# Single-pass warm-up products and a new hand-written order for the first phase of an mLSTM and mixture-of-experts kernel

## The chip, the core and the metric

The kernel runs on one core of a Trainium2 chip. The metric is device time in microseconds (us) of one execution; lower is better. One execution was taken apart by the hardware profiler, and all rows below come from it. The engines are named as the profile names them: PE (TensorE matmul), PEld (its weight loads, which overlap PE), DVE (VectorE), ACT (ScalarE), POOL (GpSimd) and SP (SyncE, which here only starts DMA transfers). SPq and POOLq are the queues on which these two start transfers.

## The reference

Three layers follow each other. The first is a gated recurrent attention (mLSTM) over 4 batches, 8 heads, 768 positions and head size 40; the second is a plain feed-forward layer over the 3072 tokens; the third sends each token to one of 8 experts.

```python
def _attn_ref(q, k, v, i_gate, f_gate, o_gate):      # B, H, S, D = 4, 8, 768, 40
    for t in range(S):
        m_new = np.maximum(f_gate[:, :, t] + m, i_gate[:, :, t])
        f_stab = np.exp(f_gate[:, :, t] + m - m_new)
        i_stab = np.exp(i_gate[:, :, t] - m_new)
        C = f_stab * C + i_stab * np.einsum('bhd,bhe->bhde', vt, kt)
        n = f_stab * n + i_stab * kt
        h_tilde = np.einsum('bhde,bhe->bhd', C, qt)
        denom = np.maximum(np.abs(nq), 1.0)          # nq = n . qt
        y[:, :, t] = o * h_tilde / denom             # o = sigmoid(o_gate)

def _moe_ref(x, w_in, w_out, alpha):                 # 3072 x 320 -> 2048 -> 320
    h = x @ w_in
    g = np.maximum(h, 0.0) + alpha * np.minimum(h, 0.0)
    return g @ w_out

def _moe2_ref(x, w_gate, w_output_gate, w1, w2):     # 8 experts, 320 -> 1024 -> 320
    e_idx = np.argmax(x @ w_gate, axis=1)            # one expert for each token
    for e in range(E):
        h = np.maximum(x[mask] @ w1[e], 0.0)
        out[mask] = gate_w[mask, None] * eom[mask, e, None] * (h @ w2[e])
```

## The kernel before

**First phase.** The attention is worked in 24 units: 4 batches times 6 chunks of 128 positions. A unit has about a dozen steps: loads of q, k, v and gates, the scores (`att_s`, on PE from `q` and `k`), their masking by `D` (`att_e` on ACT and POOL), the product with the values (`att_b`), the reading and the update of the running state (`att_h`, `att_d`), the division (`att_y`) and the transposition into `xTs` (`att_c`). Every three units fill a block of 384 tokens. A block then runs through the feed-forward layer in 16 slices of 128 hidden columns: `ffn1` (code F, eight products of 384 columns), the two-sided activation on ACT and DVE, `ffn_split` (code g, a copy on ACT and a subtraction on DVE), and `ffn2` (code S, nine products of 336 columns into three accumulators). There are 8 blocks, so 128 of each of F, g and S. Full precision comes from splitting a number into a high and a low half and multiplying them one by one.

Beside this the first phase decodes and splits the feed-forward weights (`dec_*`, `split_*`, `gate_w`), and reads the 64 pieces of the expert weights, splits them and stores both halves in the DRAM tensor `scr` (`expert_load`, `expert_split`, `expert_store`). Near its end it picks the expert of each token (`block_out`, `block_out2`), stores the rows in the DRAM tensor `x1d`, and sorts the tokens by expert (`route_*`), which gives `tok`, the list of rows for each slot of 128 tokens, and `roff`, the place of each slot's weights.

**Second phase.** Some 28 slots of 128 tokens follow (`slot_x`, `slot_1`, `slot_t`, `slot_2`, `slot_out`). Each gathers its rows from `x1d` by an indirect DMA on POOL and multiplies them by one expert's weights, which lie in the large buffer `ring`. The same buffer holds the feed-forward weights in the first phase, so the 33 `early_load` steps (code ld) bring the first three experts into parts of it as these come free. Slot 0 is worked inside the first phase (`first_rows`, `first_x`, `first_1`, `first_t`, `first_2`), since its rows are known from the first seven blocks; `first_set` clears its row buffer, which is one of the five buffers of the tag `D`. The slots from 1 on need the rows of all blocks in `x1d`, the whole of `tok`, and `roff`.

**What sets the order.** Nothing is scheduled by the compiler there. `ORDER` (lines 85 to 124) is a string of 1399 codes; each code calls the next step of its kind, and its instructions are put at the end of the queues of the engines it uses. Every engine, and SP for the transfers, works strictly in that order, so a step that waits holds up all that stands behind it on the same engine. The tables in `OTHER` say for which numbers of a step a subtraction or multiplication goes to the other of DVE and POOL.

**Warm-up products.** `warm` (line 1138) is a PE product whose result nobody reads. It multiplies `ident` by 512 columns of the constants `cst` in float32, which PE works in four passes. There are 14: three near the start, six a little later, and five single or paired ones before the first F.

Of the kernel before, what the change touches and what calls it, by code (L numbers as in the profile page):

```python
# [11 lines left out]
I32 = mybir.dt.int32  # L12
# [36 lines left out]
        0, 1, 2, 4, 5, 6, 7, 8, 11, 12, 15, 16, 17, 18, 19, 21, 23,  # L49
    ),  # L50
    "prep_kt": (
        0, 1, 2, 3, 9, 10, 12, 13, 15, 16, 21, 22,
    ),
    "att_y": (
        5, 6, 8, 9, 11, 12, 14, 16, 17, 20, 21,
    ),
# [6 lines left out]
    "split_wi": (  # L63
        0, 1, 2, 7, 9, 10, 15,
    ),
    "split_wo": (
        3, 4, 11, 13, 15,
# [18 lines left out]
lo gates_d load_gates do load_cst do load_gates lo load_wg gates pq do lo do do gw lv log do so so lg pq pq pq  # L86
pq warm warm warm gates_e do li li load_g load_g gates lk do gw di do gv pq di ae so warm warm warm warm warm
warm gates_e gw di load_sel di di lq si li di di load_g ae lg pt lo gv as as ab si load_g di do di lv sg do ay
do si gv lq lo el do li ae ad pt gw do ay do lk warm gates_d ah ay so so es gw lo di gv load_g ae do di ay ae lv
load_g ae as as do di do lq lq ah ad pt ab lk ac so ay ay ay si et ay lo as as do ah do lo gv do load_gates  # L90
gates gw warm gw ab do gv ay li lk do ay ac so lg ay gv ay lg do so di warm gw warm warm gates_e di lo ac do do
load_g load_g ae ae di si set_al1 el pq es load_g do ae lv ad lk pt as as F F load_g g ah ab gv so gw lo gates_d
li di di gv lq et g do do lv do so di si ad F log F lo do gw li di S do do g lv S so ah g lq gw di di si ay li
di di F F lg lg di S g g S ay load_g load_g pk pk lo do do as do sg si so li di F lo pt gw pk pk di di ae pt do
do pk gv ay ay si F ad ad g S g do li li di di gv S di S ah si gv di di di gw F so g pq load_g li di di gv si as
di li di S di ah li ae di lq lk F F si ab as lo do S si el g g do di do di ae as load_g ae ae di li ac es F ay
ay ay ay so F g S gw g ab ay ay ay log si di di gv li pq di ac di di S S di ay lv pt sg si lk lg si as as F ad
et load_g load_g load_g g S lk lk lo do do do ac lo lq do log do el el ae so lg do ab ay F so F gw pk as ae as
lv lv g S ay el g es pt gv load_g ae gw et el es es ay ay F F ah ad ae gv pk S pk g lq ac load_g et et S g bo F
F g es lq pq ab S g el el load_g load_g ae ae as lk ay as ay S bp F g F pk pk ah lg ab es et et S S g es F F g  # L100
as ay load_g pt S lv S lg ay ay g ad pt lk F el as pk es lq lq ac g S ae ae load_g F g lq S S F pq et el es et
ay ah ad F lv pt ab el as g g S sg load_g load_g es ay ay ah F g et F S g lk pt el as pq el pk ad ay et F S g el
ay S ac F g es et ab ay ay ay ae ae ay F F es es S S lg g lv load_g ah ah el as et g lk lv el S bo F as g ay et
es ac pq pk S lk F g load_g F ab ay ay et S g lq es et log ae F F load_g S S g el bp S ae g el el as F lv lg g
ac S lk lg lg F g F as S ae g pq pt es et S ay ay ay es F g F S S ad ad log g pt F ah pk sg es ad ab load_g F et
g ah ae S g as S lq lg lg as pq et F g lv el ac F ay es S S g el es pk ae load_g ay ay load_g F ay et et g S S
bo el el F lk ac es es ae el ab S pt et g as as pk es lq et F S F lv g g ad lq el ab pq F F S el et g g es S es
ah S ae load_g load_g lv et el ae ae F g F g ay ay ay el S pt ad pt load_g F F g S et lk ay es load_g g as F as
pk sg S g es ac pq pt S lk el ab F g et et load_g ay ay es F ay S lk g F lq ay S ay el el ae es ae ah as g et et
el F es et S g S ac lg el bp F F es as ad g pk es S g ae S S bo el ab ah lv load_g load_g et et lk lg el el F g  # L110
load_g F S g es F log pq F et g S g S bp lq F g es es ay el ah as ay et et ae ay S S F as pk F g g ay ay ae ab
pq F F lq S S S g g el F ac g F el es lv lv sg ay S ay lg es g F pt lg S g ay ac ay ay S et es F et et ay as ae
log g F as pq pk el lk el el S S S ac g F g ad ad pt es et es ab F F S g g ay et as ah es ay load_g ay S bo ay
ae F F S S g g ac el es et load_g lg el es S load_g et F ae as el g lq S F g F ad g es ab ay ay pq lk pk el sg S
S F F S g ay as et g el es load_g load_g S lv lv ae as ay et lk pt ah et es F pk S F load_g g g ae ad ab el es F
g ay S lq pq ay ay F el S et el es lq g pt load_g load_g ac F et ay F et ah ae as as pk S pq g g ab el el ac lv
bp ay F lq S g es ad F S et es F S g g S load_g es et et el bo F g F ae S S S g ae S ay lk ay ay lg lg el es pt
# [1167 lines left out]
```

## Time and profile before

| what | value |
| --- | --- |
| median of 3 runs | 833.61 us (832.91 to 836.97) |
| the profiled execution | 830.8 us, of which 829.0 us are its span |
| PE busy | 782.5 us, 94% of the span |
| PEld busy | 734.1 us, 89% |
| DVE busy | 466.8 us, 56% |
| ACT busy | 399.0 us, 48% |
| POOL busy | 265.0 us, 32% |
| mean granted clock of PE | 0.953 of full speed |

Busy time is a mean over a start-up of some 90 us, a long middle, the change between the phases at about 558 to 600 us, and the second phase. A busy PE is not PE at full speed: the granted clock has two levels, 2.4 GHz (1.00 in the rows) and 1.2 GHz (0.50), and a row between them is a stretch with both. The profile's chain of work that ended last is only two short pieces on POOL here, so the order of events is read from the timeline and the waits.

### The profile page before, as it was taken

Reading aid. Unit: us, or ns where it says so; the run is one execution under the profiler, and the core shown is the slowest. Engines: PE = TensorE matmul, PEld = TensorE weight load, DVE = VectorE, ACT = ScalarE, POOL = GpSimd, SP = SyncE. Lnnn points to the kernel's source line nnn. Section 1 sums busy time; section 2 is a strip of 40 time slices with the busy share of each in tenths; the row PEclk is TensorE's granted clock in tenths of the full one; section 3 lists DMA queues with packets and bytes.
Section 4 is the critical chain, followed back from the end, with each engine's and each line's share of the span. In section 5 each row is a group of like instructions: output and inputs, shape, how many; then the busy total and the mean of one; then the engine's idle time right before and its main releaser. Section 6 shows DMA issues by size and latency. Waiting matters only on the chain. (4 is left out here: it accounts for less than half of the span.)

```text
span 829.0 us, 15173 instructions
## 1 busy us (share of the span) xinstructions
PE 782.5 (94%) x4819; PEld 734.1 (89%) x4819; DVE 466.8 (56%) x1137; ACT 399.0 (48%) x859; POOL 265.0 (32%) x274
## 2 busy tenths in 40 slices
PE   5999999998999999999999999997699999999995
PEld 2897999998999998999998899996599999989994
DVE  5767889775767765757777576854223232323231
ACT  2624665746666757557666564331233232323331
POOL 1224233334444444354236342100222121212221
PEclk9657999999999999999999999997799999999998
DMA  7747658879799998996987976986554662771100
GB/s 221 238 145 222 190 152 283 284 229 303 238 317 287 287 292 265 308 307 235 292 264 250 304 274 240 317 319 235 183 204 183 231 266 88 293 291 30 41 13 19
DMA packets 84272, 189.45 MB, mean 229 GB/s; under 512 B 8786, under 2 KB 39567, under 8 KB 82914
## 3 DMA queue, kind: packets, MB, share of 16 engines
q1 hardware_dynamic: 80802, 179.74, 65.9%
q0 software_dynamic: 3392, 8.71, 3.3%
q8 instruction: 44, 0.72, 0.4%
q14 instruction: 34, 0.28, 0.1%
HBM read 267.71 MB, written 55.59 MB: 390 GB/s over the span
## 5 line engine op out<-in xcount | busy, mean ns | idle before, releaser
L830 PE MATMUL ph<-ring 128*128 128x384 f32 x1024 | 202.7, 345 | 7.6 <-DVE ring L846 7.2
L830 PEld LDWEIGHTS ph<-ring 128*128 128x128 f32 x1024 | 179.3, 191 | 11.8 <-DVE ring L846 11.1
L858 PE MATMUL acc<-ring 128*128 128x336 f32 x384 | 122.9, 325 | 2.2 <-ACT ring L845 1.5
L859 PE MATMUL acc<-ring 128*128 128x336 f32 x384 | 119.6, 317 | 0.0
L839 DVE SCALAR_TENSOR_TENSOR ph<-v,al,ph 128x384 f32<-128x384 f32 x128 | 78.2, 617 | 61.5 <-ACT v L838 60.7
L290 PE MATMUL po<-ring,hh 128*128 (+1 forms) x448 | 99.2, 308 | 1.2 <-DMA ring<-scr 1.0
L290 PE MATMUL p<-ring,xh 128*128 (+1 forms) x336 | 97.0, 412 | 0.6 <-issue 0.6
L1087 POOL TENSOR_TENSOR er<-er,ring 128x768 fp32r<-128x768 f32 (+1 forms) x39 | 67.7, 1742 | 92.2 <-ACT ring L1086 82.8
L390 DVE TENSOR_SCALAR yo<-po,xg 128x320 f32<-128x320 f32 x27 | 14.9, 551 | 143.6 <-PE po L290 143.6
L846 DVE TENSOR_TENSOR ring<-ph,ring 128x384 fp32r<-128x384 f32 x128 | 70.6, 555 | 40.9 <-ACT ring L845 39.0
L838 ACT ACTIVATE v<-ph 128x384 f32<-128x384 f32 x128 | 61.7, 486 | 60.0 <-PE ph L830 59.5
L845 ACT ACTIVATE ring<-ph 128x384 fp32r<-128x384 f32 x128 | 62.0, 488 | 55.7 <-DVE ph L839 52.4
L391 POOL DMA_INDIRECT out_dram<-yo,tok x28 | 28.5, 1019 | 168.9 <-DVE yo L390 161.7
L861 PE MATMUL acc<-ring 128*128 128x336 f32 x384 | 80.3, 317 | 0.0
L290 PEld LDWEIGHTS po<-ring,hh 128*128 128x128 f32 x448 | 75.8, 187 | 4.1 <-ACT hr L358 1.4
L290 PEld LDWEIGHTS p<-ring,xh 128*128 128x128 f32 x336 | 63.7, 197 | 13.9 <-issue 1.0
L858 PEld LDWEIGHTS acc<-ring 128*128 128x128 f32 x384 | 72.3, 188 | 4.0 <-ACT ring L845 2.1
L372 ACT ACTIVATE hh<-p 128x512 fp32r<-128x512 f32 x56 | 30.5, 597 | 89.0 <-PE p L369 89.0
L859 PEld LDWEIGHTS acc<-ring 128*128 128x128 f32 x384 | 72.2, 188 | 0.0
L358 ACT ACTIVATE hr<-p 128x512 f32<-128x512 f32 x56 | 33.6, 600 | 74.9 <-PE p L290 70.1
L290 PE MATMUL po<-ring,hl 128*128 (+1 forms) x224 | 69.1, 309 | 0.3 <-DVE hl L373 0.3
L1086 ACT ACTIVATE ring<-er 128x768 fp32r<-128x768 f32 (+1 forms) x64 | 50.0, 788 | 29.5 <-DMA er<-in_ew_dram 11.8
(193 smaller groups left out, 1307.9 us busy)
## 6 DMA issues: line engine op xcount, KB each, us to landing
ring<-scr SPq DMA_DIRECT2D x28, 3072.0 KB
ring<-scr SPq DMA_DIRECT2D x28, 2560.0 KB
ring<-scr SPq DMA_DIRECT2D x33, 512.0 KB
D<-gd SPq DMA_DIRECT2D x48, 256.0 KB
er<-in_ew_dram SPq DMA_DIRECT2D x32, 384.0 KB
scr<-ring SPq DMA_DIRECT2D x32, 384.0 KB
scr<-er SPq DMA_DIRECT2D x32, 384.0 KB
er<-in_ew_dram SPq DMA_DIRECT2D x32, 320.0 KB
```

Of the source, the lines that this page charges most:

```text
L290: mm = T.matmul(o_, lhsT, r, start=start, stop=stop)
L358: A.activation(hr[:, hf * 512 : (hf + 1) * 512], ph, AF.Relu)
L830: T.matmul(ph[:, :384], wi_[i][lo][:, wc], xTs[n % 2][:, xc], start=(a == 0), stop=(a == len(PASSES) - 1),)
L838: A.activation(v, ph[:, :384], AF.Relu, scale=-1.0)
L839: V.scalar_tensor_tensor(ph[:, :384], v, al1[:, i : i + 1], ph[:, :384], ALU.mult, ALU.add)
L845: A.activation(gh, v, AF.Copy)
L846: V.tensor_tensor(gl, v, gh.bitcast(F32), ALU.subtract)
L858: T.matmul(ac, gh[:, sl], hi, start=(i == 0), stop=False)
L859: T.matmul(ac, gh[:, sl], lo, start=False, stop=False)
L861: T.matmul(accs[n][t][:, :NO], gl[:, t * P : (t + 1) * P], hi, start=False, stop=(i == NFC - 1))
L1086: A.activation(eh[:, :n], st[:, :n], AF.Copy)
L1087: engine(G, V, "expert_split", x).tensor_tensor(st[:, :n].bitcast(F32R), st[:, :n], eh[:, :n].bitcast(F32), ALU.subtract)
```

## The change

Two things are changed. `warm` multiplies two parts of a region of `ring` that is cleared once by POOL at the start. The region is the first 640 columns of `xt_odd`, which the first phase writes only with its fourth unit; the type is float32r, which PE works in one pass. There are 23 such products in place of 14. And `ORDER` and `OTHER` are written anew: all 1399 steps and nine more `warm`, in another order.

```diff
 OTHER = {
     "expert_split": (
-        0, 3, 8, 12, 15, 20, 23, 28, 29, 32, 34, 37, 38, 41, 43, 44, 45, 46, 47, 53, 56, 58, 59, 60, 62,
+        0, 6, 7, 8, 11, 12, 14, 15, 16, 19, 21, 23, 25, 27, 30, 33, 34, 35, 36, 37, 39, 41, 43, 48, 49,
+        50, 52, 54, 55, 57, 58, 59, 61, 62, 63,
     ),
     "prep_q": (
-        3, 4, 5, 6, 7, 9, 10, 11, 12, 16, 17, 18, 19, 20, 21, 22, 23,
+        3, 4, 5, 6, 7, 11, 12, 15, 16, 22, 23,
     ),
...
 ORDER = """
-lo gates_d load_gates do load_cst do load_gates lo load_wg gates pq do lo do do gw lv log do so so lg pq pq pq
...
-ld ld ld ld ld route_c ld ld first_t ld first_2 ld ld ld bp route_d
+pq lo do do do pq lk lo gates_d ah load_gates load_cst do do do lv gw warm load_gates load_wg gates warm warm lo
...
+first_x ld ld S S ld ld bo ld ld ld bp first_1 first_t route_b route_c ld first_2 ld es es route_d et et ld ld
...
-    "warm": ("warm", zip(range(14))),
+    "warm": ("warm", zip(range(23))),
...
+        odd0 = carved[0]
         xt_odd = carve(5, 384)
...
+        idle = ring[:, odd0 : odd0 + 5 * P]
+        G.memset(idle.bitcast(I32), 0)
+
         def warm(i):
 
-            T.matmul(ps_h(f"warm_{i}"), ident, cst[:, :512], start=True, stop=True)
+            T.matmul(ps_h(f"warm_{i}"), idle[:, :P], idle[:, P:], start=True, stop=True)
```

The other tables of `OTHER` change in the same way. Counted over the whole program, DVE takes over from POOL 10 of the subtractions of `expert_split`, 6 of `prep_q`, 3 of `prep_k`, 4 of `split_wi` and 2 of `split_wo`, and gives it 2 of `prep_kt` and 2 of `att_y`. Lines behind 428 move down by three, and behind 1138 by six.

At the start, on SP's queue, in the kernel before (`D` is the decay matrix loaded from `gd`, `gd<-G` stores its source once DVE has made `G` for the second part of the gates, `k_0` and `q_0` are the first unit's operands):

```order
L687 DMA D_0_172<-gd 128x4x128
L687 DMA D_1_174<-gd 128x4x128
L516 DMA gd<-G_177 32x256
L456 DMA k_0_190<-in_ks_dram 40x1024
L1132 DMA sel<-in_selc_dram 32x360
L449 DMA q_0_248<-in_qs_dram 40x1024
```

The same place now:

```order
L519 DMA gd<-G_137 32x128
L578 DMA r_wo_153<-in_wo_dram 128x640
L452 DMA q_0_155<-in_qs_dram 40x1024
L690 DMA D_0_157<-gd 128x4x128
L578 DMA r_wi_159<-in_wi_dram 128x768
L690 DMA D_1_161<-gd 128x4x128
L578 DMA r_wi_169<-in_wi_dram 128x768
L452 DMA q_1_171<-in_qs_dram 40x1024
L519 DMA gd<-G_174 32x256
```

The loads of `q_0` and (further up) `k_0` stood behind the second store to `gd`; now they stand ahead of it.

At the end of the first phase, on PE, before (`acc` are the accumulators of `ffn2`, so the first two rows end the last S; `xt` is the transposition of slot 0's gathered rows `x`, `ranks` is `route_b`, `p_0_0` is `first_1`):

```order
L861 MATMUL acc_1_5739<-ring 128x336
L861 MATMUL acc_2_5740<-ring 128x336
L338 MATMUL xt_6206<-cst,x_5796 128x128 x3
L994 MATMUL ranks<-rb,cst 128x32
L999 MATMUL ranks<-oh_all,cst 128x24
L999 MATMUL ranks<-oh_all,cst 128x16
L999 MATMUL ranks<-oh_all,cst 128x8
L1004 MATMUL ranks<-oh_all,cst 128x24
L290 MATMUL p_0_0_6223<-ring,xh_6210 128x512 x3
```

The same place now, where `ph` is the last F:

```order
L833 MATMUL ph_6160<-ring 128x384 x8
L340 MATMUL xt_6180<-cst,x_3580 128x128 x3
L861 MATMUL acc_0_5775<-ring 128x336
L862 MATMUL acc_0_5775<-ring 128x336
L861 MATMUL acc_1_5776<-ring 128x336
```

The transposition of slot 0's rows stood behind the last S; now the last two S stand behind it. The `ranks` products stand behind `first_1` and `first_t` now.

On DVE, in the same stretch, before (`tok` is written by `route_c`, `hl` belongs to `first_t`, `ex`, `sm`, `z`, `zs` and `xr` to the last `block_out2`, whose rows then go to `x1d`):

```order
L988 TENSOR_TENSOR tok<-rb 128x31
L373 TENSOR_TENSOR hl_6302<-p_0_0_6303,hh_6301 128x512
L373 TENSOR_TENSOR hl_6302<-p_0_1_6310,hh_6301 128x512
L894 TENSOR_TENSOR ex_6346<-lg_6185,mx_6198 128x24
L897 TENSOR_REDUCE sm_6349<-ex_6346 128x3
L899 TENSOR_TENSOR z_6351<-lg_6185,oh_all 128x24
```

And now, where `oh_all` is the last result of `block_out`:

```order
L889 TENSOR_TENSOR oh_all<-q_7_6227,m_7_6230 128x24
L897 TENSOR_TENSOR ex_6236<-lg_6212,mx_6225 128x24
L900 TENSOR_REDUCE sm_6239<-ex_6236 128x3
L902 TENSOR_TENSOR z_6241<-lg_6212,oh_all 128x24
L904 TENSOR_REDUCE zs_6243<-z_6241 128x3
```

`block_out2` stood behind the whole of `route_c` and `first_t`; now it follows `block_out` at once, and `first_t` and `route_c` come after it.

## Rows read from the trace of the kernel before

**Rows 1.** Windows: length, busy by engine (instructions), PE clock, DMA share, GB/s.

```profile
40.00:60.00 20.00, 20.00 (x87) 18.10 (x86) 13.30 (x34) 3.80 (x12) 4.34 (x7) 0.50 0.43 137
...
100.00:540.00 440.00, 426.98 (x2795) 417.62 (x2795) 309.64 (x737) 270.91 (x582) 174.03 (x168) 1.00 0.85 272
...
560.00:580.00 20.00, 14.39 (x84) 12.40 (x85) 8.09 (x39) 3.20 (x7) 1.37 (x6) 0.74 0.62 232
...
600.00:829.00 229.00, 218.73 (x1334) 200.86 (x1333) 64.63 (x131) 68.81 (x129) 54.27 (x53) 0.99 0.41 152
```

**Rows 2.** Waits of PE over the span: in total us, times, longest us.

```profile
PE ph L830 <- DVE ring L846: 7.2, 8, 1.9
PE xt L338 <- DMA x<-x1d,tok: 6.4, 1, 6.4
PE xt L338 <- DMA xg<-x1d,tok: 6.2, 1, 6.2
```

**Rows 3.** Timeline of PE at the start: start, us, line, what, records.

```profile
9.22 4.90 PE L1140 MATMUL warm<-cst 128*128 128x512 f32 x6
13.96 0.25 PE L532 MATMUL pe_ek<-cst,w 96*128 96x96 f32 x1
...
22.30 2.38 PE L707 MATMUL ps<-q,k 40*128 40x128 f32 x16
...
64.71 3.61 PE L1140 MATMUL warm<-cst 128*128 128x512 f32 x4
...
71.49 3.09 PE L830 MATMUL ph<-ring 128*128 128x384 f32 x16
```

**Rows 4.** Timeline of the other engines at the start, in brackets the idle time before.

```profile
10.94 0.31 ACT L529 ACTIVATE w<-w 32x128 f32<-32x128 f32 x1
...
14.24 0.26 DVE L533 COPY EKT<-pe_ek 128x96 f32<-128x96 f32 x1 [3.99 <-PE pe_ek L532]
...
18.42 0.36 SPq L449 DMA_DIRECT2D q<-in_qs_dram  x1
```

**Rows 5.** Groups by line: shapes, count, busy us, mean ns, idle before.

```profile
L1087 POOL TENSOR_TENSOR er<-er,ring 128x768 fp32r<-128x768 f32 x22 | 40.9, 1860 | 40.6 <-ACT ring L1086 31.2 <-DMA scr<-ring 8.4 <-DMA er<-in_ew_dram 0.9
...
L665 DVE TENSOR_TENSOR ring<-k,ring 40x1024 fp32r<-40x1024 f32 x6 | 9.2, 1536 | 3.4 <-ACT ring L663 3.4
...
L1087 DVE TENSOR_TENSOR er<-er,ring 128x768 fp32r<-128x768 f32 x10 | 9.5, 956 | 3.9 <-ACT ring L1086 3.7
...
L657 DVE TENSOR_TENSOR ring<-q,ring 40x1024 fp32r<-40x1024 f32 x3 | 3.7, 1223 | 0.5 <-ACT ring L655 0.4
```

**Rows 6.** Timeline from the first phase's end to slot 1, all engines.

```profile
555.16 0.68 PE L978 MATMUL pfirst<-rb,bh 128*128 128x1 f16 x21
...
557.90 1.23 POOL L328 DMA_INDIRECT x<-x1d,tok  x1 [27.14 <-DVE ring L846]
...
558.17 0.62 PE L861 MATMUL acc<-ring 128*128 128x336 f32 x3
...
565.19 0.87 PE L338 MATMUL xt<-cst,x 128*128 128x128 f32 x3 [6.39 <-DMA x<-x1d,tok]
...
568.06 0.18 DVE L1018 TENSOR_TENSOR rb<-ranks,oh_all 128x24 f32<-128x24 f32 x1 [0.69 <-PE ranks L1004]
...
570.12 2.76 PE L290 MATMUL p<-ring,xh 128*128 128x512 f32 x6
...
570.58 0.95 DVE L1036 TENSOR_TENSOR a<-cst,rb 128x768 f16<-128x768 f32 x1
...
574.16 0.77 PE L1044 MATMUL ptok<-a,bh 128*128 128x32 f16 x24
...
575.41 0.19 DVE L988 TENSOR_TENSOR tok<-rb 128x31 int32<-128x31 f32 x1
...
577.29 0.17 DVE L894 TENSOR_TENSOR ex<-lg,mx 128x24 f32<-128x24 f32 x1
...
583.40 1.03 POOL L328 DMA_INDIRECT xg<-x1d,tok  x1 [18.11 <-DMA x1d<-xr]
...
586.50 0.90 PE L338 MATMUL xt<-cst,xg 128*128 128x128 f32 x3 [6.17 <-DMA xg<-x1d,tok]
...
587.98 1.65 PE L290 MATMUL p<-ring,xh 128*128 x3 [0.58 <-issue]
```

More of the change, by code (lines that the diff above doesn't have):

```diff
@@ L85 @@
 ORDER = """
-lo gates_d load_gates do load_cst do load_gates lo load_wg gates pq do lo do do gw lv log do so so lg pq pq pq
[L87 to L110, printed above, removed]
@@ L121 @@
-F pt bh bh S g bh bh bh es ld F g ad et et bp S F F g bh bh S g S ld ld F F ld ld S ld ld g S bh g F g F g S
-route_first ld ld S F F g g S S bh bh bh bh F route_first2 first_rows S g S bo first_x route_b first_1 ld ld ld
-ld ld ld ld ld route_c ld ld first_t ld first_2 ld ld ld bp route_d
+pq lo do do do pq lk lo gates_d ah load_gates load_cst do do do lv gw warm load_gates load_wg gates warm warm lo
+lq load_g li load_g gates_e li lq gates so so do do do gv gw gv gw so ae load_g load_g load_g di load_sel di di
@@ new lines @@
+gates_e si di log di pt ad ae li di ae ae as pq si as lg sg di di di si lg ab ay lo lo lo do do do do gv gw li
+lk lk do do ah gw ay gates_d so so do do di di lv do so pt load_gates warm warm ay di gv warm ay as ad warm ae
+warm warm lv el pk es as lg si warm ah load_g lo do do do li warm lq ac et lq ab ay ay ay gv warm ay warm ae as
+as lo lo gates gw gv do load_g load_g do do ab ay ay so gw gw pt set_al1 ay lk lk so do ac gv warm warm ay
+load_g load_g warm warm pq pq gates_e do warm warm do ac ad ae ae as so di di warm warm as lv pt ae el warm F
@@ new lines @@
+load_g warm li es et lo pq ah lg F lk di g gv lo ab gw gates_d g di di di F si ad lg gv S si do do do g F do do
+do li li g ah gw so lo F lv S di di so di lg lq gw di di si do g F S S pt di li do do as si log log g so F di
+load_g di gw ay ay di ay sg ay gv lo do g do do li S si S ad pk pk ae ae ae di as di F di F gw gv lq so lq g li
+li di di gv si di S g di di si as li ad di di load_g ae di di S gv F F el es li as si ab lo g g ah ah pt do do
+load_g si ae ay pk ay di lv di lk do S S so load_g di si ac F pq F g ay ay pq ab ay ay S gw li di di di S ae lv
@@ new lines @@
+lq li di ac ay g di ay F di et load_g as as si S ac lo lo lk do si do ab ay ay pk do pq do g sg gv lv do el pk
+pk F pt gw do so so F es load_g gv el el gw g et load_g es S ae ay lk ad ae ay as as gv g F lq S S bo g lg lg F
+lk el ah ab lv ay et g pk pk es et es S et ae as as F F S g g pt ad pt pk F ac el el ay el g load_g es load_g
+load_g F ah ad S S g lq lq pq lv F et es ay ay F g et el ab lg lg lk bp log ay ay S S g ac ay lv ae ae F pt g S
+S ay el as F es es g ah ad pt F g as pk pq S S et es ae F F et ah ab ay g S load_g ae sg as as lq pq S g lk F g
@@ new lines @@
+lq ad log S el el es ay ac F pk ab et g S es load_g load_g ae pt ay ay load_g F lg F g g ae ay ah ah as et S S
+bo el es F as pq el et et ac g F ay S S lg g lq el ay ay load_g load_g F g F g es es lg lk pk S lv lv pt S F F g
+ab g et et lk ae el load_g load_g S F g ae ad lv es et as F el ad bp S g F as pq pk S S el el S F es g ac g ab
+ay S et es ay ay ae F g ah ay lq lq F S ae lv g es as as F g lk pk pq S S pt F F g et et el ac S lg es g el el
+load_g et es et ad pt lg ae el load_g lk ay S F F g es ay ae S bo g as ay lk F sg ay ab el ay ay lv S S g es as
@@ L124 @@
+first_x ld ld S S ld ld bo ld ld ld bp first_1 first_t route_b route_c ld first_2 ld es es route_d et et ld ld
+ld
 """
```

35 lines of the change are left out of this document (20 added, 15 removed).

## Prediction

> **What bounds the kernel now.** I read the windows first, since the busy share is a mean over unlike stages. From 100 to 540 us PE is busy for 426.98 of 440 us at full clock, and DVE, the next, for 309.64 [rows 1]: there PE is the bound, and only its 13.0 us of idle time can be had. From 600 us on PE is busy for 218.73 of 229 us at 0.99 of the clock; the change touches nothing there, so each microsecond won or lost before slot 1 arrives at the end. Two stretches stand out. From 40 to 60 us PE is busy all the time, but at a clock of 0.50 [rows 1]. And from 560 to 580 us it is busy for 14.39 of 20 at a mean clock of 0.74. The waits of PE name the second stretch: 6.4 us for slot 0's rows and 6.2 us for slot 1's, beside 7.2 us in eight waits of F for the DVE subtraction that frees its PSUM buffer [rows 2]. So I go through start, middle and end in turn.
>
> **The start.** Three four-pass warm-ups run from 9.22 to 13.96 us, 1.58 us each. The first gate transposition (`pe_ek`) stands behind them; its input was ready at 11.25 (10.94 and 0.31), and DVE sat idle for 3.99 us until it came [rows 3, 4]. DVE's second gate part, the store to `gd`, and behind this on SP the load of `q_0` at 18.42 follow one another, and unit 0's scores start at 22.30. A single-pass product of 512 columns took 0.46 us at the low clock (2.76 us for six, [rows 6]). Three of them end at 9.22 + 1.4 = 10.6, before the input is ready, so `pe_ek` runs some 2.7 us sooner (13.96 less 11.25). The loads of `q_0` and `k_0` go ahead of the second `gd` store and can't eat this up; PE still has unit 0 behind the second `pe_ek`, so the 2.7 us pass on to it. Clearing the zeroed region is one POOL instruction at the start, while POOL waits for its first data: nothing.
>
> From the first scores to the first F, PE's steps are the same in both orders but for one state product moved ahead and the warm-ups: five four-pass ones before, nineteen single-pass ones now. At the low clock that is 5 x 1.7 = 8.5 us (1.58 from the first three, 1.8 from the two at 64.71) against 19 x 0.46 = 8.7 us: even. What is open is whether they lift the clock. At 71.49 the clock was up: two F of eight products with 384 columns took 3.09 us [rows 3], where at the low clock's price they would take 16 x 0.46 x 384/512 = 5.5. One bound is that the clock now rises only with the F themselves: a loss of 2.4 us on these and as much again on what stands between them, about 5 us. The other is that it is up from 24 to 64 us: then DVE, busy for 13.30 of 20 us at the low clock, allows two thirds of the time, a gain of 40 x (1 - 0.665) = 13 us. I take 0, since that row shows this same mixture of steps at 0.50 with warm-ups strewn in.
>
> **The middle.** The same F, g, S and attention steps stand in another order, and PE's total there is the same. DVE takes over ten subtractions of `expert_split` at 0.956 us, six of `prep_q` at 1.223 and three of `prep_k` at 1.536 [rows 5]: 9.6 + 7.3 + 4.6 = 21.5 us; the smaller moves go both ways. POOL loses 1.86 us for each large piece. The cover is DVE's free time, 130 us of those 440, which falls to about 109. If the cover is missed, all 21.5 us come out as waits of F; if the new order removes every wait, 13 us are won. I take 0. One row buffer of tag `D` is now held by slot 0's rows from about the middle on, so twelve later loads of `D` have four buffers instead of five; they stand behind the product that frees theirs on PE in the new order, so SP would wait little there.
>
> **The end.** Let T be the end of the last S, 558.8 us (558.17 and 0.62). Slot 1's first product came at 587.98, 29.2 us later [rows 6]. That time was: 6.4 us for the gather of slot 0; 9.0 us for `xt`, `ranks` and `first_1` up to `ptok` at 574.16, with PE at the low clock after that pause; 6.2 us for `ptok`, `first_t` and `first_2`; 6.2 us for slot 1's gather; 1.5 us for its transposition. Slot 1's gather started only at 583.40, although `tok` was written at 575.6: POOL waited 18.11 us for the stores to `x1d`, since `block_out2` came on DVE at 577.29, behind everything else.
>
> In the new order this is taken apart. From `pfirst` at 555.16 to the use of slot 0's rows at 565.19 were 10.0 us. Three F and three S now stand between these on PE; at 1.5 us an F (half of 3.09) and about the same for an S, by columns, that is 9.0 us, so PE waits about 1.0 us ahead of the last two S instead of 6.4 behind them. After T: `first_1`, sixteen products, 3.7 us at full clock; `first_t` about 2 (eight transpositions by the three `xt` in 0.87, with ACT between); `ranks` 1.5; the DVE chain of `route_c` 3.5 (568.06 to 571.53); `ptok` and `tok` 1.4; POOL 0.2; the gather 3.1 (583.40 to 586.50); the transposition 1.5. That is 16.9 us after T, and 17.9 with the wait. `block_out2` is over before `first_t`, so its stores leave ahead of `tok`. `first_2` lies beside the gather; `route_d`, which now follows two expert subtractions (2 x 0.956), ends with the gather, just covered. At the low clock throughout, `first_1`, `first_t`, `ranks` and `first_2` add 3.7, 1.3, 1.4 and up to 3 us: 27 us. So the end gains between 2 and 11.3 us. I take 10.5, near the full clock, since PE goes in without the pause after which the row shows it slow.
>
> **The sum.** 2.7 + 0 + 0 + 10.5 = 13.2 us. Against the profiled execution's 830.8 this is 817.6; the median of the runs shown is 2.8 above that execution, so I forecast 820.4, say 820.
>
> **Rivals.**
> *The warm-ups lift the clock early.* For it: they are many and stand close together, two to four in a row, where the low-clock stretch is. Against it: the strewn four-pass ones did not hold it up. Price: up to 13 us more, 807 to 813 us. The Trainium skill (TensorE: Matmul & The Clock Gate, Part 1) says that activity of the array releases the throttle; by that rule zeroed operands count like any, and this result would be the likelier one. No product of zeros stands in this trace, so it neither agrees nor disagrees.
> *The end's gain is eaten.* The 28 early loads stand ahead of the stores to `x1d` on SP. Slot 0's gather took 7.3 us from its start at 557.90 while DMA was busy (share 0.62 of the window, all of it at its front), slot 1's 3.1 us when it was idle. Before, 33 loads kept the engines busy up to 0.62 x 20 = 12.4 us into that window; five fewer of 0.5 MB at 232/0.62 = 374 GB/s end 7 us sooner, about T + 7, so the stores should land before `tok` at T + 12. If they don't, or if slot 0's rows keep the last two S waiting, the end gives 2 to 5 us and the whole is 826 to 832. The Trainium skill (DMA: Bandwidth & Descriptors, Queues, rings and completion order) says that a ring's descriptors are consumed in order, so that the stores can't overtake the loads; by it this case stands or falls with the backlog. The 7.3 us fit it.
> *DVE becomes the bound (slower).* The moved 21.5 us land on the engine that F already waits for. From the point at which some 13 of the 21.5 come out as waits of F, the start's and the end's gain is gone; at all of it the time is 833.6 - 13.2 + 21.5 = 842. For it: the eight waits of 7.2 us are waits for just this engine. Against it: DVE is busy for only 70% of the middle, 75% then.
> *It does not do what it says.* `pe_ek` waits for something else and slot 1 for another transfer: 833 us, with little chance, since both waits are named in the rows.
>
> **How the numbers follow.** The forecast gets 0.55, with 814 to 826 as its own range; the early clock 0.15; the eaten end 0.15; DVE as the bound 0.12; no effect 0.03. The range from 809 to 833 leaves out the lower half of the early clock and DVE's case, about 0.2. A measurement can tell about 0.5% from no change, 4.2 us: faster means below 829.4, slower above 837.8. Faster takes the forecast, the early clock and half of the eaten end, 0.77; slower 0.10, most of DVE's case; same the rest, 0.13.
>
> **What would show it.** The start is right if the first scores come near 19.6 us and the first F near 69, with the clock still at 0.50 from 40 to 60; a clock above 0.7 there is the first rival. The end is right if PE's two waits for gathered rows sum to under 5 us in place of 12.6 and slot 1's first product follows the last S by 17 to 20 us; POOL's wait for the stores to `x1d` should no longer release that gather. If the waits of F for DVE grow from 7.2 to over 15 us, or PE's busy time from 100 to 540 us falls below 415, the slow rival is at work. The prediction is wrong if slot 1 still comes more than 25 us after the last S, or if the middle moves by more than 5 us.

## The result

The changed kernel takes 812.54 us in the median (808.89 to 816.02, four runs) against 833.26 for the kernel before (832.05 to 836.97): a ratio of 0.974, 95% interval 0.969 to 0.980. Runs that lie over 1.5% above the fastest of their kernel are left out of the ratios. The forecast was 820, range 809 to 833. The profiled execution took 808.89 us with a span of 807.0, against 830.8 and 829.0 before, so 22.0 us are to be found between the two traces. Four marks cut both spans in the same places: the start of the sixth F (the 41st record of F, eight to one F), the end T of the last S, and slot 1's first product. Ahead of the sixth F PE has the same products in both orders, but for the warm-ups.

| stretch (us) | before | after | difference | forecast |
|---|---|---|---|---|
| span's start to the sixth F | 92.2 | 92.9 | +0.7 | -2.7 |
| sixth F to T | 466.6 | 455.5 | -11.1 | 0 |
| T to slot 1's first product | 29.2 | 19.3 | -9.9 | -10.5 |
| from there to the end | 241.0 | 239.3 | -1.7 | 0 |

The total came near the forecast, and the end too; the other two terms didn't, and their errors cancel only in part. Of the 1.7 us in the last row 1.1 are PE's busy time, 230.75 and 229.68 us for the same 1380 products: in the first 10 us behind slot 1's first product the clock is 0.71 before and 0.86 after. The windows of the changed kernel, with the columns of [rows 1]:

```profile
40.00:60.00 20.00, 19.46 (x104) 17.01 (x103) 16.98 (x42) 6.75 (x17) 3.33 (x6) 0.79 0.54 171
100.00:540.00 440.00, 435.25 (x2887) 427.63 (x2885) 324.00 (x767) 270.45 (x587) 142.89 (x157) 1.00 0.87 278
560.00:580.00 20.00, 17.65 (x85) 15.22 (x84) 7.29 (x24) 4.63 (x9) 6.63 (x6) 0.82 0.81 290
```

The 0.79 from 40 to 60 us flatters: the trace's first entry for the clock is at 44.8 us, and what lies ahead of it reads 1.00, though eight scores at 39.47 took 2.07 us there, the price of the low clock. With those 4.8 us at 0.50 the stretch comes to 0.67.

From 100 to 540 us PE now idles 4.7 us in place of 13.0, although DVE carries 14 us more work and POOL 31 us less. The waits of PE over the whole span, with the columns of [rows 2]:

```profile
PE pw L636 <- DVE f_wo L599: 8.7, 2, 7.3
PE pe_ek L535 <- ACT w L532: 3.9, 3, 2.9
PE ptok L1047 <- DVE a L1039: 3.8, 1, 3.8
PE xt L340 <- DMA xg<-x1d,tok: 1.7, 1, 1.7
```

The 7.2 us of F behind its DVE subtraction and the 6.4 us for slot 0's rows [rows 2] are gone from the head of this list (F's is 1.1 now); slot 1's 6.2 us are 1.7. Two new waits have come: 2.9 us of the second `pe_ek` at the start, and 3.8 us of `ptok` at the end.

**The start after.** PE's timeline, and ScalarE's and DVE's behind the wait, with the columns of [rows 3, 4]:

```profile
9.94 0.42 PE L535 MATMUL pe_ek<-cst,w 96*128 96x96 f32 x1 [0.45 <-ACT w L532]
...
19.97 0.58 PE L535 MATMUL pe_ek<-cst,w 96*128 96x96 f32 x2 [2.89 <-ACT w L532]
...
22.15 3.78 PE L710 MATMUL ps<-q,k 40*128 40x128 f32 x16
...
17.91 0.41 DVE L525 TENSOR_TENSOR w<-w,G 32x256 f32<-32x256 f32 x1
...
17.91 1.27 ACT L698 ACTIVATE D<-D,EKT 128x128 f32<-128x128 f32 x4
19.08 0.40 ACT L531 ACTIVATE w<-G 32x256 f32<-32x256 f32 x1
19.50 0.41 ACT L532 ACTIVATE w<-w 32x256 f32<-32x256 f32 x1
```

The first `pe_ek` comes 4.0 us sooner (9.94 for 13.96). But the second one, ahead of unit 0 on PE, waits for exponentials that stand behind weight decoding on DVE (up to 17.91) and behind unit 0's decay on ScalarE (up to 19.08). The scores start at 22.15, 0.15 us sooner than before, and their sixteen products take 3.78 us where they took 2.38 [rows 3].

**The end after.** The chain that ended last, in pieces (start, us, what), then POOL's and PE's timeline; T is 548.4:

```profile
552.06 4.80 DMA x1d<-xr
...
559.52 0.04 DVE tok L991
```

```profile
560.48 1.59 POOL L330 DMA_INDIRECT xg<-x1d,tok  x1 [10.72 <-DVE er L1090]
...
553.28 0.31 PE L997 MATMUL ranks<-rb,cst 128*128 128x32 f32 x2
...
558.24 0.80 PE L1047 MATMUL ptok<-a,bh 128*128 128x32 f16 x24 [3.76 <-DVE a L1039]
...
566.52 0.52 PE L340 MATMUL xt<-cst,xg 128*128 128x128 f32 x3 [1.74 <-DMA xg<-x1d,tok]
567.65 1.62 PE L292 MATMUL p<-ring,xh 128*128 x3 [0.62 <-DMA ring<-scr]
```

The second of the three stores to `x1d`, the one in this chain, lands at 556.86, and the packets of the third end at 558.5, ahead of the token list at 559.7. So they no longer hold slot 1's gather, as they did for 18.11 us [rows 6]. But the gather itself takes longer. From its start to the transposition of its rows were 3.1 us before and are 6.0 now; the windows of these two stretches, before and after, show the DMA engines at a share of 0.27 and of 0.86:

```profile
583.40:586.50 3.10, 0.00 (x0) 0.00 (x1) 0.00 (x0) 0.00 (x0) 2.49 (x3) 0.53 0.27 68
```

```profile
560.48:566.52 6.04, 4.30 (x21) 4.07 (x19) 2.91 (x14) 0.00 (x0) 4.58 (x4) 0.74 0.86 284
```

And slot 1's first product waits another 0.62 us for its weights (`ring<-scr`), whose load stands behind two expert subtractions and `route_d`, as the last row of the timeline says.

### The profile page after: what moved, and what is told of

Same layout as the page of the kernel before. It is cut to its first block, busy times and chain, and to the rows that moved or that the text cites. A ratio compares the mean times of both kernels' runs of the same rounds, so it can differ in the third digit from the quotient of the medians.

```text
span 807.0 us, 15128 instructions
## 1 busy us (share of the span) xinstructions
PE 770.0 (95%) x4814; PEld 730.2 (90%) x4814; DVE 482.0 (60%) x1158; ACT 392.7 (49%) x855; POOL 225.3 (28%) x254
## 4 chain that ended last, share of the span: by engine, by line
PE 70%; DMA 16%; DVE 7%; ACT 2%; issue 2%; SPq 1%; POOL 1%; POOLq 0%; DVEq 0%; ACTq 0%
PE ph L833 17%; PE p L292 11%; PE po L292 10%; PE acc L861 5%; PE acc L862 5%; PE acc L864 5%; DMA ring<-scr 4%; PE pa L777 4%; PE ps L710 3%; PE p L371 3%; DMA r_wi<-in_wi_dram 1%; PE pwg L646 1%; DMA scr<-er 1%; DMA x1d<-xr 1%; PE pd L749 1%
## 5 line engine op out<-in xcount | busy, mean ns | idle before, releaser
L833 PE MATMUL ph<-ring 128*128 128x384 f32 x1024 | 200.5, 343 | 1.1 <-DVE ring L849 1.1
L292 PE MATMUL po<-ring,hh 128*128 (+1 forms) x448 | 101.2, 313 | 0.7 <-DMA ring<-scr 0.7
L292 PE MATMUL p<-ring,xh 128*128 (+1 forms) x336 | 93.9, 402 | 0.6 <-DMA ring<-scr 0.6
L292 PEld LDWEIGHTS p<-ring,xh 128*128 128x128 f32 x336 | 61.7, 190 | 13.1 <-ACT xh L343 0.8
L1090 POOL TENSOR_TENSOR er<-er,ring 128x640 fp32r<-128x640 f32 (+1 forms) x29 | 50.0, 1727 | 53.0 <-ACT ring L1089 44.7
L698 ACT ACTIVATE D<-D,EKT 128x128 f32<-128x128 f32 x192 | 60.2, 392 | 8.5 <-DMA D<-gd 8.2
```

The lines of the kernel that those rows point to most:

```text
L292: mm = T.matmul(o_, lhsT, r, start=start, stop=stop)
L698: A.activation(d[:, j], d[:, j], AF.Exp, bias=EKT[:, c, i + j : i + j + 1])
L833: T.matmul(ph[:, :384], wi_[i][lo][:, wc], xTs[n % 2][:, xc], start=(a == 0), stop=(a == len(PASSES) - 1),)
L1090: engine(G, V, "expert_split", x).tensor_tensor(st[:, :n].bitcast(F32R), st[:, :n], eh[:, :n].bitcast(F32), ALU.subtract)
```

## The experiments

Each kernel was cut at the same marks in its profiled execution. "New order" means that of the changed kernel, "old" that of before; the ratio is to the kernel before, run beside it on the same chip. Each stretch is one execution.

| kernel | first scores | first F | sixth F | to T | to slot 1's product | to the end | ratio, 95% |
|---|---|---|---|---|---|---|---|
| before | 22.3 | 71.5 | 92.2 | 466.6 | 29.2 | 241.0 | 1 |
| after | 22.2 | 72.1 | 92.9 | 455.5 | 19.3 | 239.3 | 0.974 (0.969 to 0.980) |
| warm_only | 23.8 | 75.3 | 96.1 | 467.1 | 27.3 | 242.8 | 1.008 (1.005 to 1.011) |
| no_warm | 22.6 | 74.2 | 95.4 | 452.9 | 18.7 | 239.1 | 0.978 (0.973 to 0.984) |
| old_other | 22.9 | 80.0 | 102.4 | 459.6 | 19.7 | 238.6 | 0.989 (0.984 to 0.995) |
| new_other_b | 21.9 | 70.3 | 94.2 | 477.1 | 28.8 | 241.1 | 1.018 (1.012 to 1.024) |
| after_again | 23.1 | 79.4 | 100.2 | 452.9 | 18.8 | 239.3 | 0.981 by the medians of all four runs, 0.973 by those of the two that the ratios keep |
| start_fix | 23.2 | 76.2 | 98.8 | 450.8 | 18.6 | 239.1 | 0.976 (0.969 to 0.983) |
| warm_data | 22.0 | 81.5 | 102.2 | 452.3 | 20.1 | 239.4 | 0.976 (0.969 to 0.984) |
| warm4 | 24.7 | 85.9 | 109.5 | 454.2 | 18.8 | 239.3 | 0.991 (0.987 to 0.995) |
| old_end | 23.3 | 78.5 | 99.3 | 453.7 | 23.9 | 240.1 | 0.986 (0.981 to 0.992) |
| new_end_b | 22.1 | 71.4 | 91.7 | 475.8 | 19.6 | 238.6 | 0.998 (0.994 to 1.002) |
| combo | 21.8 | 70.2 | 91.3 | 454.8 | 18.0 | 239.4 | 0.976 (0.971 to 0.982) |
| combo2 | 22.4 | 71.4 | 92.5 | 454.6 | 17.3 | 239.6 | 0.969 (0.964 to 0.973) |

### The warm-ups alone, in the old order (warm_only)

```diff
-            T.matmul(ps_h(f"warm_{i}"), ident, cst[:, :512], start=True, stop=True)
+            T.matmul(ps_h(f"warm_{i}"), idle[:, :P], idle[:, P:], start=True, stop=True)
```

> The kernel before with only the warm-up products of the change (14 single-pass products over the zeroed region, order and DVE/POOL tables of before). Theory A, the one of the prediction (the first gate transpose stands behind three four-pass products): first scores about 2.7 us earlier than 22.3, the time 828 to 831. Rival B (the start is paced by VectorE and ScalarE, as the changed kernel's 2.9 us wait of the second gate transpose suggests): first scores within 1 us of 22.3, the time 831 to 836. If the shorter products also lose a clock rise that the four-pass ones bought between 60 and 70 us, first feed-forward product later than 71.5 and the time over 836.

Measured: 836.97 us, slower by 0.5 to 1.1%. Of the three cases of the text the last came: the first F at 75.3 and a time over 836. PE's timeline at its start, against that of before ([rows 3] and the second fence):

```profile
11.68 0.42 PE L533 MATMUL pe_ek<-cst,w 96*128 96x96 f32 x1 [0.59 <-ACT w L530]
...
13.88 2.93 PE L1144 MATMUL warm<-ring 128*128 128x512 f32 x6
21.51 0.58 PE L533 MATMUL pe_ek<-cst,w 96*128 96x96 f32 x2 [4.70 <-ACT w L530]
...
23.78 3.76 PE L708 MATMUL ps<-q,k 40*128 40x128 f32 x16
```

```profile
15.14 5.42 PE L1140 MATMUL warm<-cst 128*128 128x512 f32 x12
20.92 0.39 PE L532 MATMUL pe_ek<-cst,w 96*128 96x96 f32 x2 [0.36 <-ACT w L529]
```

The first `pe_ek` does come 2.3 us sooner (11.68 for 13.96), and the second one doesn't (21.51 for 20.92). The four-pass warm-ups of before fill PE's wait for the second gate part almost wholly (0.36 us of it are left); behind them the scores run at the full clock, sixteen in 2.38 us. The short ones leave 4.70 us of waiting, and the scores behind them take 3.76 us. At the sixth F this kernel is 3.9 us late, and it stays so. So the first warm-ups of before were not a cost that held `pe_ek` back: PE had nothing else to do, and in this order they paid for themselves in clock.

### The new order without warm-ups (no_warm), with other numbers (warm_data), with the long ones (warm4), and again (after_again)

no_warm leaves out all 23 codes `warm` of the order, of which a piece stands here; warm_data and warm4 follow:

```diff
-load_cst do do do lv gw warm load_gates load_wg gates warm warm lo
+load_cst do do do lv gw load_gates load_wg gates lo
```

```diff
-        G.memset(idle.bitcast(I32), 0)
+        G.memset(idle.bitcast(I32), 0x3F9DC000)
```

```diff
-            T.matmul(ps_h(f"warm_{i}"), idle[:, :P], idle[:, P:], start=True, stop=True)
+            T.matmul(ps_h(f"warm_{i}"), ident, cst[:, :512], start=True, stop=True)
```

> The changed kernel without its 23 warm-up products. Theory A (they stand where TensorE would wait anyway, and the full clock from 43.5 to 52.8 us is what they buy): first feed-forward product 1 to 4 us later than 72.1, the time 813 to 817. Rival B (they only cost TensorE time): 23 products at 0.43 to 0.79 us are 10 to 18 us, of which some part returns: first feed-forward product 2 to 8 us earlier, the time 805 to 811.

> The changed kernel with the number 1.23 in the place of zero in the region that the warm-up products read. Theory A (the clock follows what TensorE does, not the numbers in it): clock and time as in the changed kernel within 1 us of the first feed-forward product. Rival B (products of zeros lift the clock less): full clock earlier than 43.5 us, the first feed-forward product 2 us or more earlier, the time 2 to 8 us shorter.

> The changed kernel with the warm-up products of before in its 23 places (four passes, on the constants). Theory A (the longer products buy full clock from about 14 us on, as in the kernel before; the experiment with the short products in the order of before lost 4 us by the first feed-forward product): the first feed-forward product at 66 to 71, the time 803 to 809. Rival B (they cost 0.4 to 0.8 us more each, 23 of them, and the gate transposes wait behind them): first feed-forward product at 75 to 82, the time 812 to 820.

> The changed kernel once more, beside the three kernels that follow on the same chip: a ratio of 0.969 to 0.980, first scores near 22, first feed-forward product near 72.

Measured: 811.22 us without warm-ups, 812.50 with 1.23 in the place of zero, 822.68 with the long ones, and 813.71 (801.4 to 818.5) for the changed kernel again. The repeat tells most, since it is the same program. PE at 44 us in the first execution, and in the second; then the first F of the second:

```profile
42.72 1.63 PE L1146 MATMUL warm<-ring 128*128 128x512 f32 x3
44.28 1.39 PE L710 MATMUL ps<-q,k 40*128 40x128 f32 x8
```

```profile
44.27 1.63 PE L1146 MATMUL warm<-ring 128*128 128x512 f32 x3
45.83 2.07 PE L710 MATMUL ps<-q,k 40*128 40x128 f32 x8
...
53.56 0.73 PE L1146 MATMUL warm<-ring 128*128 128x512 f32 x2
...
79.42 2.73 PE L833 MATMUL ph<-ring 128*128 128x384 f32 x8
```

In the first, the eight scores behind the three warm-ups already run faster; in the second the same eight take 2.07 us, and of the warm-ups only those at 53.56 do. There the clock falls back at once: from 54.7 to 82.0 us it is granted at 0.50, with PE busy for 26.23 of the 27.30 us. The first F starts at 72.1 in one execution and at 79.4 in the other. So one trace of this start isn't the start. Four executions share the new start but for the numbers in the region (after, after_again, warm_data, old_end): the sixth F at 92.9, 100.2, 102.2 and 99.3, mean 98.7. Four share the old one (before, new_end_b, combo, combo2): 92.2, 91.7, 91.3, 92.5, mean 91.9. The new start is some 7 us later on the mean and spreads over 9 us, the old one over 1.2.

Without warm-ups the first F came at 74.2, 2 us later than in the one execution of the changed kernel and 5 sooner than in the other, and the time is the same within the spread: neither theory's microseconds can be told from nothing. With 1.23 in the region the first F came at 81.5, and no full clock is on the trace ahead of it, so rival B's earlier rise didn't come; theory A's 1 us can't be tried on a start that moves by 7 us by itself. In the time the numbers make no difference that shows. The Trainium skill says that activity of the array releases the throttle (TensorE: Matmul & The Clock Gate, Part 1); zeros and 1.23 gave the same time, which agrees, but not one run shows the 23 short products to shorten this kernel. The long ones in their 23 places are the worst of all, beyond even rival B's figures: the first F at 85.9 (rival B: 75 to 82), the sixth at 109.5, the first scores at 24.7.

### The second gate part ahead of the decoding (start_fix)

```diff
-gates so so do do do gv gw gv gw so ae load_g load_g load_g di load_sel di di gates_e si
+gates gates_x so so do do do gv gw gv gates_y gates_e gw so ae load_g load_g load_g di load_sel di di si
```

`gates_x` is the addition of `gates_e` on DVE, `gates_y` its two exponentials on ScalarE.

> The changed kernel with the second gate part's addition on VectorE and its two exponentials on ScalarE ahead of the weight decoding and of the copies for unit 0's decay, and its transposes behind the second gate product. Theory A (the 2.9 us wait of the second gate transpose is what ate the start): first scores at 19 to 20.5 us, first feed-forward product 1.5 to 3 us earlier than in the changed kernel, the time 1.5 to 3 us shorter. Rival B (the next piece of the start is late anyway: decay copies, q, the decoded weights, or the low clock): first feed-forward product and time within 1 us.

Measured: 810.70 us, first F at 76.2: nothing that can be told from the changed kernel, rival B. PE's timeline:

```profile
15.58 0.58 PE L543 MATMUL pe_ek<-cst,w 96*128 96x96 f32 x2 [1.01 <-ACT w L535]
16.78 0.90 PE L644 MATMUL pw<-cst,f_wo 128*128 128x128 f32 x3 [0.61 <-DVE ring L657]
21.67 1.59 PE L757 MATMUL pd<-kv,kt 128*120 128x123 f32 x6 [3.99 <-POOL kt L684]
23.18 3.78 PE L718 MATMUL ps<-q,k 40*128 40x128 f32 x16
```

The transposes do come at 15.58 instead of 19.97, and the next piece waits instead: the state product for `kt` from POOL, 3.99 us. The first scores come at 23.18, where theory A said 19 to 20.5. The 2.9 us were one of several chains that end at the same time.

### Tables and order of the middle (old_other, new_other_b)

old_other has all seven tables of `OTHER` as they were before; new_other_b has the new ones in the old order. The first line of one of them, in old_other:

```diff
     "expert_split": (
-        0, 6, 7, 8, 11, 12, 14, 15, 16, 19, 21, 23, 25, 27, 30, 33, 34, 35, 36, 37, 39, 41, 43, 48, 49,
...
+        0, 3, 8, 12, 15, 20, 23, 28, 29, 32, 34, 37, 38, 41, 43, 44, 45, 46, 47, 53, 56, 58, 59, 60, 62,
```

> The changed kernel with the DVE/POOL tables of before (order and warm-ups of the change). Theory A (the middle's 11 us come from the new order of the steps): the time 810 to 815, TensorE idle from 93 us to the last S at most 7 us. Rival B (they come from the 21.5 us of work that went from POOL to DVE): 820 to 825, TensorE idle there near 13 us again, waits of the feed-forward product for the split on DVE near 7 us.

> The kernel before with the DVE/POOL tables of the change (order and warm-ups of before). Theory A (the order is the cause, the tables only fit it): 831 to 838. Rival B (the tables are the cause): 821 to 826, TensorE idle in the middle 5 us and not 13.

Measured: 821.78 and 843.69 us. Neither theory holds as it was put: old_other's time is rival B's, but its middle is near theory A's, and its sixth F at 102.4 lies where the other executions of the new start have it; new_other_b is slower than either said. PE's work from the sixth F to T, with the columns of [rows 1], in before, after, old_other (new order, old tables) and new_other_b (old order, new tables):

```profile
92.20:558.80 466.60, 453.57 (x2976) 443.30 (x2974) 326.17 (x778) 283.21 (x606) 176.11 (x170) 1.00 0.85 272
```

```profile
92.90:548.40 455.50, 450.64 (x2982) 442.35 (x2980) 335.27 (x792) 276.43 (x602) 146.01 (x164) 1.00 0.87 279
```

```profile
102.40:562.00 459.60, 451.86 (x2982) 443.56 (x2981) 324.70 (x782) 276.85 (x602) 176.52 (x175) 1.00 0.86 276
```

```profile
94.20:571.30 477.10, 456.62 (x2976) 445.67 (x2974) 338.99 (x789) 283.63 (x606) 146.19 (x159) 0.99 0.83 266
```

PE idles 13.0, 4.9, 7.7 and 20.5 us. The new order alone takes 5.3 us of idle time away, the tables another 2.8 within it; in the old order the same tables add 7.5. The rest of the differences is PE's busy time for the same products, 453.57, 450.64, 451.86 and 456.62 us, and it goes roughly with the clock: in these stretches it stands at 0.50 for 3.4, 0, 3.4 and 10.2 us. In stretch lengths: the order with the old tables gives 7.0 us, the tables 4 to 7 more (455.5 here, 452.3 to 453.7 in its three other executions), and in the old order they cost 10.5. Where PE waits in the middle, with the columns of [rows 2], in old_other and in new_other_b:

```profile
PE pd L748 <- DVE kt L675: 1.5, 1, 1.5
...
PE ph L832 <- DVE ring L848: 0.4, 1, 0.4
```

```profile
PE ph L831 <- DVE ring L847: 5.8, 9, 2.2
PE acc L859 <- ACT ring L846: 4.4, 2, 3.6
PE pt L816 <- DVE hN L732: 3.1, 1, 3.1
```

The order is what removes F's wait for its subtraction: 7.2 us before, 0.4 with the old tables. Which of its moves does it isn't shown. What is left then is single waits for pieces on one engine or the other, which the tables remove if they are drawn up for that order and cause if they are not.

### The end alone, both ways (old_end, new_end_b)

```diff
-first_rows first_x ld ld S S ld ld bo ld ld ld bp first_1 first_t route_b route_c ld first_2 ld es es route_d
+first_rows ld ld S S bo first_x route_b first_1 ld ld ld ld ld route_c first_t ld first_2 ld es es bp route_d
```

new_end_b puts `route_first2`, `first_rows` and `first_x` of the old order ahead of the last products, `bp` soon behind `bo`, and `first_1` and `first_t` ahead of `route_b`.

> The changed kernel with the end of before: first_x behind the last products and the block's outputs, the stores of the last rows (bp) behind first_2 and behind the early loads. Theory A (the end's 10 us come from these moves alone): from the last S to slot 1's first product 27 to 30 us in the place of 19, the last S where the changed kernel has it, the time 8 to 11 us over the changed kernel's, a ratio of 0.984 to 0.992. Rival B (the last rows are stored late for another reason, or the gain is in the order before the last S): 21 to 24 us, the time at most 5 us longer.

> The kernel before with the interleaved end alone: the routing of the first rows ahead of four more products, first_x ahead of the last S, the stores of the last rows right behind the block's outputs. Theory A: from the last S to slot 1's first product 18 to 21 us in the place of 29, the time 7 to 11 us shorter than before, a ratio of 0.986 to 0.992. Rival B (the row gather, 5 us, is not covered by the two products that stand behind it, or waits behind loads on another queue): 23 to 27 us, the time 2 to 6 us shorter.

Measured: 817.60 and 827.70 us. In old_end slot 1 comes 23.9 us after T, theory A said 27 to 30; by this stretch rival B holds. The ratio of 0.986 lies in theory A's range, but this execution also has a late start (sixth F at 99.3). POOL's timeline:

```profile
544.17 1.23 POOL L328 DMA_INDIRECT x<-x1d,tok  x1 [35.05 <-DVE ring L847]
...
569.84 1.03 POOL L328 DMA_INDIRECT xg<-x1d,tok  x1 [15.33 <-DMA x1d<-xr]
```

T is 553.0 here. Slot 0's rows are asked for 8.8 us ahead of it, since the routing of the first rows stands earlier in the new order; before, 0.9 us ahead [rows 6]. So that wait, 6.4 us, is gone even with `first_x` behind the last S, and the moves undone here are worth the other half: 23.9 less 19.3 is 4.6 us, with the stores to `x1d` holding slot 1's gather again.

new_end_b does shorten the end to 19.6 us, theory A, and yet gains 0.2% with an interval over zero. Its stretch to T is 9.2 us longer. PE there:

```profile
557.24 0.96 PE L976 MATMUL pfirst<-rb,bh 128*128 128x1 f16 x4 [2.25 <-DVE bh L962]
558.07 0.63 PE L856 MATMUL acc<-ring 128*128 128x336 f32 x1
558.49 0.48 PE L857 MATMUL acc<-ring 128*128 128x336 f32 x1
```

The routing that I moved up now waits 2.25 us for DVE's `bh`, and the S behind it run at the low clock (0.48 us a product; the mean of that line over the changed kernel is 0.33). Of the 9.2 us some 4.7 lie behind POOL's last `y` (at 507.06 us here, 503.11 before), where the edit is. The other 4.5 lie ahead of it, in an order that is the same as before: PE is busy there for 402.86 us in the place of 398.97, with as many products (2628), and idles only 0.6 us more. The clock is what differs: 0.50 for 13.7 us in this execution, in four pieces, and for 3.4 in that of before.

### Old start, new rest (combo, combo2)

combo takes order, tables and warm-ups of before up to the first F, then the steps of the new order that are not yet done, and puts the rank products ahead of slot 0's products; combo2 moves five early loads behind the stores.

The end of the changed kernel and of combo, then of combo and of combo2:

```diff
-first_x ld ld S S ld ld bo ld ld ld bp first_1 first_t route_b route_c ld first_2
+first_x ld ld S S ld ld bo ld ld ld bp route_b first_1 route_c first_t ld first_2
```

```diff
-first_x ld ld S S ld ld bo ld ld ld bp route_b first_1 route_c first_t ld first_2
+first_x ld ld S S bo bp ld ld ld ld ld route_b first_1 route_c first_t ld first_2
```

> Order, tables and four-pass warm-ups of before up to the first feed-forward product, then order and tables of the change, and at the end the rank products of the last rows ahead of slot 0's products instead of behind them. Theory A (the start of before is as good or better, the middle's 12 to 14 us and the end's 10 us hang on the later part of the order alone, and the end waits for the ranks): the sixth feed-forward product near 92 us, from there to the last S 451 to 456, from the last S to slot 1's first product 16 to 18, the time 800 to 808, a ratio of 0.963 to 0.973. Rival B (the middle is paid by the start: buffers and loads that the new start puts ahead): from the sixth feed-forward product to the last S 460 or more, the time 812 or more.

> The last kernel (start of before, later part of the change, ranks ahead of slot 0's products) with five early loads of 512 KB moved from ahead of the stores of the last rows to behind them. Theory A (the stores, 7.15 us from issue to landing in that kernel and 4.80 in the changed one, stand behind these loads, and the gather of slot 1's rows waits for them and not for the token list, which is ready 3 us earlier): the stores land in 3 to 5 us, slot 1's gather starts at most 1.2 us after the token list, from the last S to slot 1's first product 15 to 16.5 us in the place of 18.0, the time 2 to 3 us shorter, 803 to 806, ratio 0.966 to 0.974. Rival B (the loads are what slot 1 needs next: moved behind the stores they arrive later than its rows): slot 1's first product waits for the load instead, 17.5 us or more, the time within 1 us of the last kernel's or longer.

Measured: 806.84 us (805.6 to 812.7) and 805.56 (803.7 to 808.6). combo does what theory A said stretch by stretch: 91.3, 454.8, 18.0. So the middle's gain doesn't hang on the new start, and the old start comes some 7 us sooner here too. The times don't show those 7 us: the ratio of 0.976 is above the 0.963 to 0.973 of the text, and overlaps with the changed kernel's. combo2's 0.969 (0.964 to 0.973) overlaps with it at the edge; against the eight runs of the changed kernel (801.4 to 818.5, median 813.3) the six of combo2 have a median some 8 us lower. They ran at different times, and the medians of the kernel before beside them go from 829.7 to 833.3 too, so I take combo2 as the likely better kernel, with that reserve.

What combo2 tells of the stores: the chain of combo, and of combo2.

```profile
550.30 7.15 DMA x1d<-xr
...
558.29 4.56 DMA xg<-x1d,tok
```

```profile
555.46 0.20 DVE tok L988
...
556.42 6.37 DMA xg<-x1d,tok
```

With the loads ahead of them the stores took 7.15 us and slot 1's gather started at 558.29, behind them. With five loads behind them the packets of the stores end at 553.6, and the gather starts 0.8 us after the token list, as theory A said. But the gather itself then takes 6.37 us, beside the loads, where it took 4.56: slot 1 comes 17.3 us after T, 0.7 sooner than in combo, not 2 to 3; that is near rival B's 17.5, though slot 1 waits for its rows there and not for a load. The Trainium skill says that DMAs from different issuing engines run on the same 16 DMA engines and interleave (DMA: Bandwidth & Descriptors, Issuing engines are not separate DMA queues); the 6.37 us agree with that, as do the 6.0 of the changed kernel and the 3.1 us where few transfers ran beside the gather.

## Why the prediction was right, and where it was wrong

- **The start, -2.7 us: wrong.** `pe_ek` did come sooner, by 4.0 us. The step that failed is "PE still has unit 0 behind the second `pe_ek`, so the 2.7 us pass on to it": I had followed SP's queue past the moved steps, and not DVE's and ScalarE's, where decoding and decay copies now stood ahead of the second gate part. In warm_only, too, the first `pe_ek` came 2.3 us sooner and the second 0.6 later. start_fix shows that not even this wait was the only one.
- **The clock of the start, taken as 0 between -5 and +13 us: wrong on the losing side.** The sign that I had set for the first rival, a clock above 0.7 from 40 to 60 us, isn't there: the 0.79 is 0.67 when its unrecorded part is counted as low. In the second execution the clock rose later still. On the mean of four executions each the new start loses about 7 us (98.7 against 91.9), somewhat beyond my bound of 5. The step that failed counted the warm-ups' columns as even, 8.5 against 8.7 us, between first scores and first F; it left out those ahead of the first scores, which in the old order filled a wait and gave the full clock behind it. warm_only puts that at 3.9 us in the old order. What makes up the rest of the 7 us isn't shown: in the new order neither leaving the warm-ups out nor long ones brought the old start back.
- **The middle, 0: wrong in size.** It gave 11.1 us in the profiled pair (13 to 14 in the other executions): 8.2 of idle time out of the 13 that could vanish, and 2.9 of busy time, which goes at least in part with the clock. The step that failed is "I take 0": I had set the bound of 13 us for vanished waits and that of 21.5 us for DVE's new work side by side as if they were equally likely. DVE's busy time grew by 15.2 us over the span and not by 21.5 (466.8 to 482.0), and its part in the middle (335.27 for 326.17 us) held PE up for nothing that shows in the new order. The slow rival is real, though, where the order doesn't fit: new_other_b lost 10.5 us in the middle, 7.5 of them in waits. By the prediction's own words, a middle that moves by over 5 us makes it wrong.
- **The end, -10.5 us: right.** 9.9 us in this pair, with slot 1 at 19.3 us after T for a forecast of 17.9. The term that was too small is slot 1's gather: 3.1 us, taken from a row with idle DMA engines, though slot 0's gather in the same rows had taken 7.3 beside other transfers. It took 6.0, and started 0.8 us behind the token list instead of 0.2. Against this the way to `ptok` took 9.9 us for 10.7 (its wait of 3.76 is the DVE chain that I had put at 3.5), the last transposition and its copy with the wait for the weights 1.1 for 1.5, and the 1.0 us ahead of the last two S didn't come. By old_end about half of the gain came from the earlier gather of slot 0's rows (29.2 to 23.9), half from the moves behind it, the earlier stores above all.
- **The sum: near, by compensation.** Over the executions about +7 at the start, -13 in the middle and -10 at the end, where -2.7, 0 and -10.5 were forecast, and -1.7 behind slot 1, where PE runs at the low clock for 3 us less. That the sum lies near 820 is luck in good part.
- **The eaten end:** not decisive here (the packets of the last store end 1.2 us ahead of the token list), but its mechanism appears in combo as soon as the token list is earlier, and the busy DMA engines show in the longer gather.

## What to carry to other kernels

A table that splits work between two engines belongs to the order for which it was drawn up: the same table gave 4 to 7 us in one order and cost 10 in another, so try both only together. Warm-up products are worth what the wait they fill is worth: in the old order, where PE waited anyway, longer ones that fill the wait left the clock up behind them; in the new order 23 long ones cost time, and 23 short ones gained nothing that shows. A transfer's price read where the DMA engines are idle is too small for a place where they are busy: the same gather took 3.1 and 6.0 us. Cut every trace at the same marks, and take a stretch whose clock rises at different times from several executions, not from one.

## What I had not expected of the hardware

The clock rises at different times in executions of one program: behind the warm-ups at 42.72 us in one, only at 53.56 and for a moment in the other, with the first F 7.3 us apart; with 1.23 in the region it didn't rise ahead of the first F at all. I don't know what sets it. The middle isn't free of it: the low clock lasted 13.7 us there in new_end_b and 3.4 in before, up to the same step in the same order. And the granted clock reads 1.00 ahead of the first entry in a trace, even where products run at the price of the low clock; this window of the changed kernel holds the sixteen scores that took 3.78 us:

```profile
20.00:40.00 20.00, 18.42 (x75) 16.38 (x76) 13.61 (x36) 9.92 (x27) 3.46 (x6) 1.00 0.83 242
```

Durations of like products tell the clock there, the column doesn't.
